# Loads of v, z and u issued by GpSimd instead of SP in a fused attention and token-mixing kernel

## The chip, the cores and the metric

The kernel runs on one core of one Trainium2 chip. The metric is the device time of one execution in microseconds (us); the time before is the median of three runs. The engines of the core are TensorE (PE, with its weight loads shown apart as PEld), VectorE (DVE), ScalarE (ACT), GpSimd (POOL) and SyncE (SP), which here only issues DMAs.

## What is computed

Two stages follow each other, for 8 batches of 3200 rows; u and v have 256 columns, z has 64.

```python
scores = (1 / S) * z @ z.T            # S = 3200
attn   = maximum(scores, 0) ** 2
x      = u * (attn @ v)               # first stage
wq, wk = x @ w_q, x @ w_k             # second stage
mixed  = (1 / 8) * (wq @ wk.T) @ x
out    = maximum(mixed, 0) @ w_out
```

All inputs and the output are float32 in DRAM. The kernel computes in float16 with float32 sums. In the second stage it uses wk.T @ x, which is only 64 x 256 ("heads"), so that no 3200 x 3200 matrix arises there.

## The kernel before, in words

**Tiling.** A batch has 25 tiles of 128 rows (NT). Its columns of the score matrix are cut into seven groups (NG): six of 512 and one of 128 (`widths`). For a group, score tiles of 128 rows by 512 columns are made in pairs by PE (`scores`, L307) into PSUM. `first_stage` turns a pair into g = 4 max(score, 0), on DVE (L321) or on ACT (L319). `second_stage` squares g into a float16 tile `at`, on POOL (L332) or on ACT (L330). PE then uses the `at` tiles as weights against v (`second_product`, emitted at L369) and sums into two PSUM banks `acc`. Since the score matrix is symmetric, some blocks of `at` are turned by DMA transposes on SP (L351, tiles `tt` and `ts`) and used again in a later group instead of being computed twice.

**Gate.** When a group is complete, `gate` multiplies `acc` by u into the float16 tile `x_sb`: half of it on DVE straight from PSUM (L507), the other half copied out by ACT (L506) and multiplied on POOL (L509). The last, narrow group goes by L499 to L502. `x_sb` is turned by a DMA transpose on SP (L518) for the second stage.

**Order.** Everything is written out by hand. A loop counts phases k; the engines get their instructions in the order in which the Python code emits them, and each engine and each DMA queue runs its own in that order. In a phase some two or three score pairs are made while the squares of an earlier phase are consumed (`LAG = 2`). The opening and the ending have lists of their own. `due(k, fn)` has a function called at the start of phase k; `asides` holds functions that are called later in the same phase.

**Loads.** For batch 0, z comes in four pieces through SP and is cast by three engines (`cast_first`, L121), and v comes in four pieces by DMAs that POOL issues and that cast on the way (`load_first_v`, L112). For batches 1 to 7:

- z comes in two pieces and v in seven. `load_piece` (L144 to L153) takes a float32 buffer `piece` out of the pool `pst` (three buffers), has SP load it (L147), and some phases later (3, 4 or 5) casts it into `zr` or `v_sb` (L151): on POOL in even phases, on ACT in odd ones. `V_FIRST` and `V_LATER` give the phase of each load of v and the delay of its cast.
- z is then turned by DMA transposes on SP (`turn_z`, L176), and parts are copied by ACT (`spread_z`, L184 and L188).
- u comes in float32, one piece for each group, into one of two buffers (`load_u`, L195, issued by SP). The load of the next group's u is put into `to_load` when a group begins, and it is emitted at the front of the phase after that, behind `turn_x`. Its buffer was last read by the gate of the group before.

`v_sb` has two buffers, one for each of two batches; `zr` has one.

**SP's queue.** So SP issues the transposes of `at`, `x_sb`, z and the keys (`kx`, L551), the loads of z, v and u, and the stores of the output (L740, L783, L1318). Each waits in that order for what it needs.

Of the kernel before, what the change touches and what calls it, by code (L numbers as in the profile page):

```python
# [10 lines left out]
FP32 = mybir.dt.float32  # L11
# [5 lines left out]
def kernel(  # L17
# [10 lines left out]
    nc = tc.nc  # L28
# [4 lines left out]
    P = 128  # L33
    NT = S // P
# [21 lines left out]
    px = ctx.enter_context(tc.tile_pool(name="px", bufs=7))  # L56
    pk = ctx.enter_context(tc.tile_pool(name="pk", bufs=1))
    pxt = ctx.enter_context(tc.tile_pool(name="pxt", bufs=4))
    pst = ctx.enter_context(tc.tile_pool(name="pst", bufs=3))
    pu = ctx.enter_context(tc.tile_pool(name="pu", bufs=2))  # L60
    pg = ctx.enter_context(tc.tile_pool(name="pg", bufs=7))
    pfo = ctx.enter_context(tc.tile_pool(name="pfo", bufs=2))
# [28 lines left out]
    zT, vs, us, xs, xTs, qks, ks, hacc, hss, rts, zds = ({} for _ in range(11))  # L91

    def rows(t, b):
        return t[b].rearrange("(p n) d -> p n d", n=NT)
# [5 lines left out]
    zr = pz.tile([P, NT + 1, dqk], FP16, tag="zr", name="zr")  # L100
# [37 lines left out]

    V_FIRST = [(13, 3), (14, 3), (15, 3), (16, 3), (17, 3), (18, 3), (19, 3)]
    V_LATER = [(7, 5), (9, 4), (11, 4), (13, 3), (14, 3), (15, 3), (17, 4)]

    def load_piece(k, b, src, dst, n0, nn, later):  # L144
        d = src.shape[2]
        piece = pst.tile([P, nn, d], FP32, tag="piece", name="piece")
        nc.sync.dma_start(out=piece[:], in_=rows(src, b)[:, n0 : n0 + nn, :])  # L147

        def cast():
            copy = nc.gpsimd.tensor_copy if now[0] % 2 == 0 else nc.scalar.copy  # L150
            copy(out=dst()[:, n0 : n0 + nn, :], in_=piece[:])  # L151

        due(k + later, lambda: asides.append(cast))  # L153

    def load_v(k, b, n0, nn):
        if n0 == 0:
            vs[b] = pv.tile([P, NT, D], FP16, tag="v_sb", name="v_sb")
        load_piece(k, b, v, lambda: vs[b], n0, nn, (V_FIRST if b == 1 else V_LATER)[n0 // 4][1])

    def load_z(k, b, n0, nn):  # L160
        load_piece(k, b, z, lambda: zr, n0, nn, 4)

    def z_at(b, half):
        return P if b > 0 and half == 0 else 0
# [4 lines left out]
    def turn_z(b, n0, nn):  # L173
        if n0 == 0:
            zT[b] = pzt.tile([P, S + P], FP16, tag="zT2", name="zT2")
        nc.sync.dma_start_transpose(  # L176
            out=z_tiles(b)[:, n0 : n0 + nn, 1, :],
            in_=zr[:, 2 * n0 : 2 * (n0 + nn), :].rearrange("p n k -> p (n k)"),
        )

    def spread_z(b, half, n0, n1):
        low, high = slice(0, dqk), slice(dqk, P)
        if half == 0:
            nc.scalar.copy(  # L184
                out=z_tiles(b)[low, n0 + 1 : n1 + 1, 0, :], in_=z_tiles(b)[high, n0:n1, 1, :]
            )
        else:
            nc.scalar.copy(  # L188
                out=z_tiles(b)[high, n0:n1, 0, :], in_=z_tiles(b)[low, n0:n1, 1, :]
            )  # L190

    def load_u(b, gi):
        n0, nn = starts[gi] // P, widths[gi] // P
        us[b, gi] = pu.tile([P, 4, D], FP32, tag="u_sb", name="u_sb")
        nc.sync.dma_start(out=us[b, gi][:, 0:nn, :], in_=rows(u, b)[:, n0 : n0 + nn, :])  # L195


    wqk = consts.tile([P, ND, 2, dh], FP16, tag="wqk", name="wqk")
# [590 lines left out]
    keyed, keyed_at, to_turn, to_spread, asides = [], [-9], [], [], []  # L789
    hTs, to_turn_heads = {}, []  # L790

    def due(k, fn):
        at_phase.setdefault(k, []).append(fn)
# [72 lines left out]
    def group_begun(k, b, gi):  # L866
        following = (b, gi + 1) if gi + 1 < NG else (b + 1, 0)
        if (b, gi) == (0, 0):
            due(k + 5, lambda: load_u(*following))
        elif following[0] < B:  # L870
            to_load.append(following)
        if gi == 0 and b + 1 < B:
            for i, (n0, nn) in enumerate([(0, 16), (16, NT - 16)]):
                at = k + (5 if b == 0 else 1) + i
                due(at, lambda at=at, n0=n0, nn=nn: load_z(at, b + 1, n0, nn))
            for i, n0 in enumerate((0, 5, 9)):
                due(k + (10 if b == 0 else 6) + i, lambda n0=n0: turn_z(b + 1, n0, 5 if n0 == 0 else 4))
            n = NT // 2
            for i, (half, n0, n1) in enumerate(
                [(0, 0, n // 2), (1, 0, n // 2), (0, n // 2, n), (1, n // 2, n + 1)]  # L880
            ):
                due(
                    k + (14 if b == 0 else 13) + i,
                    lambda half=half, n0=n0, n1=n1: spread_z(b + 1, half, n0, n1),
                )
            for i in range(-(-NT // 4)):
                at = k + (V_FIRST if b == 0 else V_LATER)[i][0]
                due(at, lambda at=at, i=i: load_v(at, b + 1, 4 * i, min(4, NT - 4 * i)))

    last = B - 1  # L890
    first_kx = list(kxs)
    now = [0]
    mixed_at = [-9]
    make_identity(nc, ident)
    due(3, lambda: load_u(0, 0))
    due(6, load_weights)
    due(8, load_out_weights)
# [91 lines left out]
    def opening(order):  # L989
        sc, g = {}, {}  # L990
        for word in order.split():
            what, n, by = word[0], int(word[1:2]), word[2:]
            if what == "z":
                cast_first(n, int(by[0]), by[1])
            elif what == "t":
                turn_first(n)
            elif what == "c":
                place_first(n, by)
            elif what == "v":
                load_first_v(*[(0, 4), (12, 6), (18, 7), (4, 8)][n])  # L1000
            elif what == "s":
                sc[n] = scores(2 * n)
            elif what == "e":
                g[n] = first_stage(2 * n, sc.pop(n), by == "A")
            elif what == "q":
                each(second_stage(2 * n, g.pop(n), by == "A"))
            elif what == "w":
                warm(2 * int(word[1:]))
            elif what == "u":
                load_u(0, 0)  # L1010
            elif what == "m":
                ti = [t for x in tiles[2 * n : 2 * n + 2] for t in x[2]]
                for fn in whole(second_product(0, 0, ti, n == 0, False)):
                    fn()
        return [(2 * n, g[n]) for n in sorted(g)]
# [4 lines left out]
    made_by = [4, 10, 16]  # L1020
    produced, consumed, k = 16, 6, 3
    group_begun(1, 0, 0)
    steps = 6
    across = False
# [3 lines left out]
    while groups:  # L1028
# [71 lines left out]
        b, gi = groups[0]  # L1100
        if begins:
            group_begun(k, b, gi)
            need = ends[b, gi]
            scored = tiles[consumed:need]
            scored = [t for _, _, tis in scored for t in tis]
            left = [t for t in range(NT) if t not in scored]
# [247 lines left out]
```

## Time and profile before

| | |
|---|---|
| median of 3 runs | 765.52 us (765.5 to 765.67) |
| profiled execution, first to last instruction (its own time is given only as this span) | 763.7 us |
| busy: PE / DVE / ACT / POOL | 754.3 / 461.9 / 551.1 / 537.1 us |
| mean granted clock of TensorE | 0.998 |
| DMA packets | 289614, 150.23 MB |
| read from and written to HBM | 59.38 and 26.21 MB |

How to read the lines below: in the list of groups, a row gives the line, the engine, the operation, output<-input with their shapes, the count, then the busy time in us and the mean duration of one in ns, and then the engine's idle time just ahead of them with what ended most of it. In the list of waits, a row names who waited for whom, the us in total, the times and the longest. In a timeline, a row gives the start, the time until the end of the last one, the engine, line and operation and the count. In the table of stretches, a row gives the stretch, its length, the engine's busy time (and instructions), the granted clock, the mean busy share of the 16 DMA engines and GB/s. A row of DMA issues ends with the size of one and the median us from issue to landing. SPq is SP's queue.

### The profile page before, as it was taken

The numbers are of one execution on the slowest core, as the hardware profiler recorded it, in microseconds if no ns is written. First come the engines' busy times: TensorE is split into PE (matmuls) and PEld (weight loads), VectorE is DVE, ScalarE is ACT, GpSimd is POOL, SyncE is SP. The second block draws the span as 40 slices with busy tenths as digits, with TensorE's granted clock in tenths as the row PEclk, the third lists the DMA queues.
The fourth block names the chain that finished last, engine by engine and source line by source line (L and its number), as shares of the span: only waits on it lengthen the run. The fifth ranks groups of instructions, "written<-read, shape, count | busy, mean of one in ns | idle before, by whom it ended". The sixth has DMA issues, their size and how long they took to land.

```text
span 763.7 us, 29059 instructions
## 1 busy us (share of the span) xinstructions
PE 754.3 (99%) x12888; PEld 618.0 (81%) x12888; DVE 461.9 (60%) x458; ACT 551.1 (72%) x651; POOL 537.1 (70%) x351
## 2 busy tenths in 40 slices
PE   9999999999999999999999999999999999999996
PEld 6777888888888887888888888888878888888884
DVE  7655676546755567555665557656566565755534
ACT  8666776677767777687776877759777697776555
POOL 7897797768766678676787668866688665854540
PEclk9999999999999999999999999999999999999999
DMA  8999789887999969997899998999899999798636
GB/s 178 189 197 219 187 187 192 174 181 160 206 196 233 219 166 185 221 235 195 214 177 219 243 195 181 158 228 265 135 223 189 228 250 156 161 222 193 176 74 262
DMA packets 289614, 150.23 MB, mean 197 GB/s; under 512 B 265168, under 2 KB 268752, under 8 KB 289488
## 3 DMA queue, kind: packets, MB, share of 16 engines
q1 hardware_dynamic: 288768, 146.48, 91.2%
q0 software_dynamic: 576, 1.64, 1.1%
q8 instruction: 100, 1.64, 0.9%
q14 instruction: 26, 0.21, 0.1%
q10 hardware_dynamic: 144, 0.26, 0.1%
HBM read 59.38 MB, written 26.21 MB: 112 GB/s over the span
## 4 chain that ended last, share of the span: by engine, by line
PE 97%; DVE 2%; issue 0%; DMA 0%; ACT 0%; DVEq 0%; ACTq 0%
PE acc L369 72%; PE sc L307 12%; PE fo L369 5%; PE qk L369 5%; PE mx L657 1%; DVE x_sb L507 1%; DVE fo L1312 0%; DVE g L321 0%; PE ztp L130 0%; DMA z<-in_z_dram 0%; PE qk L610 0%; DVE zT L136 0%; PE xtx L634 0%; PE hd L644 0%; ACT fo L1316 0%
## 5 line engine op out<-in xcount | busy, mean ns | idle before, releaser
L321 DVE TENSOR_SCALAR g<-sc 128x1024 f32<-128x1024 f32 x329 | 400.5, 1223 | 240.5 <-PE sc L307 225.9
L332 POOL TENSOR_TENSOR at<-g 128x1024 f16<-128x1024 f32 x229 | 431.4, 1893 | 131.1 <-DVE g L321 106.5
L369 PE MATMUL acc<-v_sb,at 64*128 64x256 f16 (+1 forms) x7187 | 461.8, 269 | 1.6 <-DVE x_sb L507 0.5
L369 PEld LDWEIGHTS <-at 64*128 64x128 f16 (+1 forms) x7187 | 353.9, 94 | 86.9 <-PE acc L369 25.4
L330 ACT ACTIVATE at<-g 128x1024 f16<-128x1024 f32 x227 | 236.1, 1056 | 14.3 <-DVE g L321 7.2
L369 PE MATMUL acc<-v_sb,tt 64*128 64x256 f16 x2552 | 178.7, 269 | 0.0
L307 PE MATMUL sc<-zT 64*128 64x512 f16 (+1 forms) x1008 | 165.3, 357 | 0.2
L319 ACT ACTIVATE g<-sc 128x1024 f32<-128x1024 f32 x127 | 130.0, 1024 | 45.5 <-PE sc L307 43.2
L369 PEld LDWEIGHTS <-tt 64*128 64x128 f16 x2552 | 130.1, 94 | 14.2
L509 POOL TENSOR_TENSOR x_sb<-gt,u_sb 128x512 f16<-128x512 f32 x48 | 61.2, 1276 | 66.2 <-ACT gt L506 61.8
L678 ACT ACTIVATE rt<-mx 128x1024 f16<-128x1024 f32 x47 | 47.9, 1024 | 32.6 <-PE mx L657 32.5
L506 ACT COPY gt<-acc 128x512 f32<-128x512 f32 x48 | 28.0, 584 | 46.5 <-PE acc L369 44.7
L307 PEld LDWEIGHTS <-zT 64*128 64x128 f16 x1008 | 51.9, 94 | 8.8 <-issue 1.7
L369 PE MATMUL fo<-wo,rt 64*128 64x256 f16 (+1 forms) x696 | 57.9, 270 | 0.0
L544 ACT CAST qk<-qk 128x512 f16<-128x512 f32 x47 | 27.5, 585 | 34.3 <-PE qk L369 31.6
L369 PEld LDWEIGHTS <-rt 64*128 64x128 f16 (+1 forms) x696 | 35.5, 94 | 15.3 <-PE fo L369 6.3
L507 DVE TENSOR_TENSOR x_sb<-acc,u_sb 128x512 f16<-128x512 f32 x48 | 33.2, 691 | 20.3 <-PE acc L369 19.5
L739 ACT ACTIVATE fo<-fo 128x1024 f32<-128x1024 f32 x39 | 39.9, 1024 | 1.9 <-PE fo L369 1.7
L369 PEld LDWEIGHTS <-x_sb 64*128 64x128 f16 x672 | 29.8, 95 | 4.5 <-PE qk L369 0.9
L369 PE MATMUL qk<-kx,x_sb 64*128 64x64 f16 x672 | 32.8, 190 | 0.0
L369 PE MATMUL qk<-xT_sb,wkq 64*128 64x512 f16 (+3 forms) x118 | 25.8, 326 | 0.0
L369 PE MATMUL qk<-xT_sb,wqk 64*128 64x384 f16 (+3 forms) x148 | 24.8, 296 | 0.0
(86 smaller groups left out, 275.2 us busy)
## 6 DMA issues: line engine op xcount, KB each, us to landing
u_sb<-in_u_dram SPq DMA_DIRECT2D x48, 512.0 KB, 5.5
out_dram<-fo SPq DMA_DIRECT2D x43, 512.0 KB, 4.1
piece<-in_v_dram SPq DMA_DIRECT2D x42, 512.0 KB, 5.2
piece<-in_z_dram SPq DMA_DIRECT2D x7, 512.0 KB, 5.2
tt<-at SPq DMA_TRANSPOSE x162, 4.6
out_dram<-fo SPq DMA_DIRECT2D x9, 256.0 KB, 2.9
piece<-in_z_dram SPq DMA_DIRECT2D x7, 288.0 KB, 4.9
u_sb<-in_u_dram SPq DMA_DIRECT2D x8, 128.0 KB, 4.2
```

What stands on the lines that cost most here:

```text
L307: nc.tensor.matmul(out=sc[:, h, at : at + w], lhsT=zT[b][half : half + dqk, ds(z_at(b, h) + ti * P, P)], rhs=zT[b][half : half + dqk, ds(z ...
L319: nc.scalar.activation(out=g[:], in_=sc[:], func=RELU, scale=GSCALE)
L321: nc.vector.tensor_scalar(out=g[:], in0=sc[:], scalar1=0.0, scalar2=GSCALE, op0=AOP.max, op1=AOP.mult)
L330: nc.scalar.square(out=out, in_=g[:])
L332: nc.gpsimd.tensor_mul(out=out, in0=g[:], in1=g[:])
L369: return nc.tensor.matmul(out=self.out, lhsT=self.lhsT(rows), rhs=self.rhs(rows), start=start, stop=stop)
L506: nc.scalar.copy(out=upper[:], in_=accs[1][:])
L507: nc.vector.tensor_mul(out=x[:, 0:n], in0=accs[0][:, 0:n], in1=ug[:, 0:n])
L509: nc.gpsimd.tensor_mul(out=x[:, n : 2 * n], in0=upper[:], in1=ug[:, n : 2 * n])
L544: nc.scalar.copy(out=qks[b, gi][:, 0:gw], in_=out)
L678: nc.scalar.activation(out=out, in_=ps[:], func=RELU)
L739: nc.scalar.mul(out=flat_out[:, sl], in_=part, mul=FINAL_SCALE)
```

## The change

The float32 staging is removed: the pool `pst`, `load_piece` and its casts. v and z are loaded by DMAs that POOL issues and that write float16 straight into `v_sb` and `zr`. u is still loaded as float32, but its DMA is issued by POOL as well. The phases in which the loads are emitted stay the same. SP's queue keeps the transposes, the first loads of z and the weights, and the stores.

```diff
-    pst = ctx.enter_context(tc.tile_pool(name="pst", bufs=3))
...
-    V_FIRST = [(13, 3), (14, 3), (15, 3), (16, 3), (17, 3), (18, 3), (19, 3)]
-    V_LATER = [(7, 5), (9, 4), (11, 4), (13, 3), (14, 3), (15, 3), (17, 4)]
-
-    def load_piece(k, b, src, dst, n0, nn, later):
-        d = src.shape[2]
-        piece = pst.tile([P, nn, d], FP32, tag="piece", name="piece")
-        nc.sync.dma_start(out=piece[:], in_=rows(src, b)[:, n0 : n0 + nn, :])
-
-        def cast():
-            copy = nc.gpsimd.tensor_copy if now[0] % 2 == 0 else nc.scalar.copy
-            copy(out=dst()[:, n0 : n0 + nn, :], in_=piece[:])
-
-        due(k + later, lambda: asides.append(cast))
-
-    def load_v(k, b, n0, nn):
+    V_FIRST = [13, 14, 15, 16, 17, 18, 19]
+    V_LATER = [7, 9, 11, 13, 14, 15, 17]
+
+    def load_v(b, n0, nn):
         if n0 == 0:
             vs[b] = pv.tile([P, NT, D], FP16, tag="v_sb", name="v_sb")
-        load_piece(k, b, v, lambda: vs[b], n0, nn, (V_FIRST if b == 1 else V_LATER)[n0 // 4][1])
-
-    def load_z(k, b, n0, nn):
-        load_piece(k, b, z, lambda: zr, n0, nn, 4)
+        nc.gpsimd.dma_start(out=vs[b][:, n0 : n0 + nn, :], in_=rows(v, b)[:, n0 : n0 + nn, :])
+
+    def load_z(b, n0, nn):
+        nc.gpsimd.dma_start(out=zr[:, n0 : n0 + nn, :], in_=rows(z, b)[:, n0 : n0 + nn, :])
...
     def load_u(b, gi):
         n0, nn = starts[gi] // P, widths[gi] // P
         us[b, gi] = pu.tile([P, 4, D], FP32, tag="u_sb", name="u_sb")
-        nc.sync.dma_start(out=us[b, gi][:, 0:nn, :], in_=rows(u, b)[:, n0 : n0 + nn, :])
+        nc.gpsimd.dma_start(out=us[b, gi][:, 0:nn, :], in_=rows(u, b)[:, n0 : n0 + nn, :])
```

The calls of `load_z` and `load_v` in `group_begun` lose the argument that told the phase.

More of the change, by code (lines that the diff above doesn't have):

```diff
@@ L874, in group_begun @@
                 at = k + (5 if b == 0 else 1) + i
-                due(at, lambda at=at, n0=n0, nn=nn: load_z(at, b + 1, n0, nn))
+                due(at, lambda n0=n0, nn=nn: load_z(b + 1, n0, nn))
             for i, n0 in enumerate((0, 5, 9)):
@@ L886, in group_begun @@
             for i in range(-(-NT // 4)):
-                at = k + (V_FIRST if b == 0 else V_LATER)[i][0]
-                due(at, lambda at=at, i=i: load_v(at, b + 1, 4 * i, min(4, NT - 4 * i)))
+                at = k + (V_FIRST if b == 0 else V_LATER)[i]
+                due(at, lambda i=i: load_v(b + 1, 4 * i, min(4, NT - 4 * i)))
     last = B - 1
```

## The prediction

> **What bounds the kernel now.** I read the page's busy line and its chain first, then the busy time of TensorE by stretches of the span, then who waited for whom on TensorE's weight loads.
>
> ```profile
> PE 754.3 (99%) x12888; PEld 618.0 (81%) x12888; DVE 461.9 (60%) x458; ACT 551.1 (72%) x651; POOL 537.1 (70%) x351
> ...
> PE 97%; DVE 2%; issue 0%; DMA 0%; ACT 0%; DVEq 0%; ACTq 0%
> ```
>
> ```profile
> 0.00:20.00 20.00, 18.77 (x207) 1.00 0.85 183
> 20.00:60.00 40.00, 39.59 (x650) 1.00 1.10 195
> 60.00:740.00 680.00, 678.83 (x11902) 1.00 0.94 196
> 740.00:763.70 23.70, 17.07 (x139) 0.95 0.62 222
> ```
>
> ```profile
> PEld L369 <- PE acc L369: 25.4, 106, 0.3
> ...
> PEld L369 <- POOL at L332: 0.2, 1, 0.2
> ```
>
> The reader is to see that the matrix engine (PE) is the bound from end to end: 97% of the chain is PE, and from 60 to 740 us it is idle for 680.00 - 678.83 = 1.17 us in all. Its larger idle times stand at the two ends, where the change moves little. A matmul's shown time covers its pipeline, so gaps of up to 0.3 us hide in "busy"; most of these are PE waiting for itself (25.4 us). GpSimd (POOL) kept PE waiting once, for 0.2 us. So removing work from other engines can give little here, and only what makes PE wait can cost. PE's own instructions and their order are the same in both compiled programs.
>
> **The change, part by part.** What leaves and what comes:
>
> ```profile
> L151 POOL CAST v_sb<-piece 128x1024 f16<-128x1024 f32 (+1 forms) x24 | 23.0, 957 | 0.0
> L151 POOL CAST zr<-piece 128x1024 f16<-128x1024 f32 (+1 forms) x7 | 6.1, 878 | 0.0
> ...
> L112 POOL DMA_DIRECT2D v_sb<-in_v_dram x4 | 2.3, 579 | 0.1
> ```
>
> ```profile
> L151 ACT CAST v_sb<-piece 128x1024 f16<-128x1024 f32 (+1 forms) x25 | 23.4, 935 | 0.0
> ...
> L151 ACT CAST zr<-piece 128x576 f16<-128x576 f32 (+1 forms) x7 | 5.8, 826 | 0.0
> ```
>
> ```profile
> u_sb<-in_u_dram SPq DMA_DIRECT2D x48, 512.0 KB, 5.5
> ...
> piece<-in_v_dram SPq DMA_DIRECT2D x42, 512.0 KB, 5.2
> piece<-in_z_dram SPq DMA_DIRECT2D x7, 512.0 KB, 5.2
> ...
> piece<-in_z_dram SPq DMA_DIRECT2D x7, 288.0 KB, 4.9
> u_sb<-in_u_dram SPq DMA_DIRECT2D x8, 128.0 KB, 4.2
> piece<-in_v_dram SPq DMA_DIRECT2D x7, 128.0 KB, 3.9
> ```
>
> *Casts.* ScalarE (ACT) loses 25 + 7 = 32 casts, 23.4 + 5.8 = 29.2 us. POOL loses 24 + 7 = 31 casts, 23.0 + 6.1 = 29.1 us. PE was not waiting for any of them, so I take no gain; at the very most it is the 1.17 us above.
>
> *Issues.* 48 + 42 + 7 + 7 + 8 + 7 = 119 loads leave SP's queue and are issued by POOL. POOL's only issues in this trace are the four first loads of v: 579 ns each on average, 528 to 720 below, at a time when few transposes ran. Under load the nearest row is that of the same u loads on SP:
>
> ```profile
> L112 POOL DMA_DIRECT2D v_sb<-in_v_dram x4: 528/534/720, 1.5 to 7.2; - x4
> ...
> DMA to landing us min/median/max: 4.5/5.4/6.4
> ```
>
> ```profile
> L195 SPq DMA_DIRECT2D u_sb<-in_u_dram x56: 338/570/1638, 14.8 to 729.9; - x56
> ...
> DMA to landing us min/median/max: 3.2/5.3/9.1
> ```
>
> So one issue costs POOL between 0.34 and 1.64 us; I take 0.58, POOL's own mean, which SP's median (0.57) agrees with. That is 119 x 0.58 = 69 us on POOL, less 29 for the casts: POOL goes from 537 to about 577 us, ACT from 551 to 522. For the steady part:
>
> ```profile
> 9.00:60.00 51.00, 45.67 (x39) 1.00 1.05 192
> 60.00:618.00 558.00, 413.21 (x256) 1.00 0.97 200
> ```
>
> From 60 to 618 us, six batches, POOL idles 558 - 413 = 145 us, 24 per batch. A batch brings 7 u + 7 v + 2 z = 16 issues, 9.3 us, and drops some 4.4 casts, 4.2 us: 5 us more against 24 idle. On average this is hidden. From 9 to 60 us only 5.3 us are idle. That is where I look closely.
>
> *The opening.* POOL squares score tiles there back to back (L332), and PE loads the squares as weights:
>
> ```profile
> 10.18 15.02 POOL L332 TENSOR_TENSOR at<-g 128x1024 f16<-128x1024 f32 x8 [2.42 <-ACT g L319]
> 25.15 1.29 POOL L509 TENSOR_TENSOR x_sb<-gt,u_sb 128x512 f16<-128x512 f32 x1
> ```
>
> ```profile
> 14.04 1.90 POOL L332 TENSOR_TENSOR at<-g 128x1024 f16<-128x1024 f32 x1
> ```
>
> ```profile
> 16.25 0.11 PEld L369 LDWEIGHTS <-at 64*128 64x128 f16 x2
> ```
>
> ```profile
> 26.38 1.91 POOL L332 TENSOR_TENSOR at<-g 128x1024 f16<-128x1024 f32 x1
> ```
>
> ```profile
> 30.04 0.10 PEld L369 LDWEIGHTS <-at 64*128 64x128 f16 x2
> ```
>
> The eight squares end at 25.20. From the third's start (14.04) the pace is (25.20 - 14.04 - 1.90) / 5 = 1.85 us. Two paces back from 14.04 is 10.34, so 0.16 us was idle ahead of the second square. In the new compiled order, u's first load stands between squares one and two; a u load and a z load between six and seven; the second z load behind the gate L509, ahead of square nine; another u load behind that. With p for an issue, squares two to six are late by p - 0.16, seven and eight by 3p - 0.16, nine by 4p - 0.16. The third square ended at 15.94, and the weight load that waits for it by the program's semaphores ran at 16.25: 0.31 us to spare. With p = 0.58 it is 0.42 late, so PE waits 0.11. The ninth ended at 28.29 and is loaded at 30.04: 1.75 to spare, 2.16 late, so 0.41, of which 0.11 was already lost: 0.30 more. **Opening: +0.41 us.** Other squares there have more to spare. VectorE (DVE) waits for squares too, because they free its output buffers:
>
> ```profile
> DVE g L321 <- PE sc L307: 225.9, 253, 2.5
> ...
> DVE g L321 <- POOL at L332: 2.5, 3, 1.0
> ```
>
> I cost that at nothing, since DVE then waits less for PE's scores (225.9 us in all). If that cover fails, DVE passes on the 1.6 us by which squares seven and eight are late.
>
> *Start of a batch.* There u, z, u are issued behind the last small gate, z again two squares later:
>
> ```profile
> 98.06 1.04 POOL L151 CAST v_sb<-piece 128x1024 f16<-128x1024 f32 x1
> 99.06 11.15 POOL L332 TENSOR_TENSOR at<-g 128x1024 f16<-128x1024 f32 x6
> ```
>
> ```profile
> 102.76 1.89 POOL L332 TENSOR_TENSOR at<-g 128x1024 f16<-128x1024 f32 x1
> ```
>
> ```profile
> 106.33 0.10 PEld L369 LDWEIGHTS <-at 64*128 64x128 f16 x2
> ```
>
> The cast (1.00 until the next start) is gone, four issues come: the third square of this run is late by 4p - 1.00 = 1.32 us and has 106.33 - 104.65 = 1.68 to spare. No stall; one begins at p = 0.67.
>
> *Waits that move.* A u load on POOL waits for both halves of an earlier gate; POOL's own half stands ahead of it in the same queue, so this is over when POOL gets there. Behind it are the squares, whose cost is counted. The load lands within 6.4 us (row above) and is read a group later, 763.7 / 56 = 13.6 us. v is loaded a batch ahead. z's transposes wait for the load instead of for a cast, which ends earlier. SP issues 119 DMAs less, and its transposes stand behind no load: I cost that at nothing, as PE's waits list no transpose.
>
> *Sum.* 763.7 + 0.41 = 764.1 us of span. The profiled execution's own time is shown only as its span; the median of the runs, 765.52, is 1.8 us above it, which I take as what lies around it. **765.9 us.**
>
> **The rivals.**
>
> *The issue costs more under load (slower).* All four of POOL's rows are from the first 8 us, and SP's issues reach 1.64. With p = 1.0, square nine is 3.84 late against 1.75: 2.1 us; the batch start at 97 us gives 4.0 - 1.0 - 1.68 = 1.3. If the six others give a quarter of that each, 2.0, the sum is 5.4: 770.9 us. It decides from p = 0.67 up. POOL as a whole would become the bound only at (24 + 4.2) / 16 = 1.76 us, above every row. Against it: POOL's and SP's medians.
>
> One mechanism would be that DVE keeps POOL from writing descriptors. In the opening both overlap:
>
> ```profile
> 7.23 0.53 POOL L112 DMA_DIRECT2D v_sb<-in_v_dram  x1
> ```
>
> ```profile
> 7.63 0.94 DVE L121 CAST zd<-z 128x448 f16<-128x448 f32 x2
> ```
>
> This cast reads and writes SBUF, and the issue was no longer than its neighbours. An issue that waited for half a DVE instruction L321 (1223 ns) would have p = 0.58 + 0.61 = 1.2, and the opening alone would cost 4.8 - 0.16 - 1.75 = 2.9. The Trainium skill, "SBUF — State Buffer", section "SBUF: two separate sides", warns of this: a DMA issued by GpSimd starves for descriptors while VectorE runs a copy in a two-port mode. By that rule the steady instructions here, which read PSUM, would leave p alone; only such casts would stretch it, and the row above shows no stretch.
>
> *The transposes suffer.* In one queue a transpose waits its turn behind a load; in two they share the DMA engines.
>
> ```profile
> q1 hardware_dynamic: 288768, 146.48, 91.2%
> ```
>
> The DMA share is 0.94 from 60 to 740 us (row above), so 6% more time per byte would make DMA the pace, and each per cent past that costs 6.8 us: 1% past is 772.7. Against it: the bytes hardly change, v's landing from POOL (5.4) is that from SP (5.2), and PE has no wait for a transpose.
>
> *The casts' time comes back.* If ACT, freed of 29 us, empties PSUM earlier, PE's idle time in the middle goes: 765.5 - 1.2 + 0.4 = 764.7; at most, with the opening's loss hidden, 764.3. More would have to come out of gaps inside PE's "busy".
>
> **How the numbers follow.** The forecast has 0.57, the dearer issue 0.24, the transposes 0.09, the casts 0.10, of which I give 0.06 to over 0.2%, since the hidden gaps are larger than the idle time. 0.2% is 1.5 us, about what a measurement of this kernel can tell from no change. The forecast and the small gain lie inside it: 0.57 + 0.04 = 0.61. Slower has 0.33, faster 0.06. The range goes from 764.5, just below the gain, to 772, which takes in the dear issue; the forecast's own is 765.3 to 766.8, for p from 0.53 to 0.72.
>
> **What would show it.** The issues on POOL should read near 0.55 us through the whole span, POOL's busy time near 577, ACT's near 522. PE's busy time from 60 to 740 us should fall short by no more than 1.5 us, and its new waits should be for "POOL at" between 16 and 31 us. It is wrong if POOL's issues are near 1 us and such waits stand at every batch start, if PE waits for transposes, or if "DVE x_sb" or "ACT gt" wait for a u load.

## The result, and the profile after

| | median us | lowest to highest | ratio to before, 95% interval |
|---|---|---|---|
| before (4 runs) | 765.51 | 765.36 to 765.67 | |
| after (4 runs) | 776.58 | 769.30 to 780.83 | 1.0131 [1.009, 1.0171] |

The change makes the kernel 1.3% slower, and its time, which was the same within 0.3 us in these runs, now scatters over 11 us. The ratios here and below leave out executions that a comparison takes for disturbed, while the medians and ranges count all, so that of a kernel that scatters by itself the median can stand higher than its ratio. The profile of after is that of its quickest run, 769.3 us with a span of 767.5: it shows 3.8 us of the loss, and a second profile, of the same kernel run again (e8, span 775.2), shows 11.5.

The page of after, its busy line and its chain, and the busy time of TensorE from 60 to 740 us:

```profile
PE 753.9 (98%) x12888; PEld 617.6 (80%) x12888; DVE 462.0 (60%) x458; ACT 526.8 (69%) x619; POOL 575.1 (75%) x439
...
PE 93%; POOL 2%; DMA 1%; ACT 1%; DVE 1%; issue 1%; ACTq 0%; DVEq 0%; POOLq 0%
```

```profile
60.00:740.00 680.00, 675.52 (x11871) 1.00 0.99 175
```

PE does the same work, but in the steady part it is idle for 680.00 - 675.52 = 4.48 us where it was idle for 1.17. That alone is 3.3 of the 3.8 us. Who waited for whom, in after:

```profile
POOL at L316 <- DMA tt<-at: 20.1, 9, 7.6
...
ACT at L314 <- DMA tt<-at: 8.4, 6, 2.0
ACT at L314 <- DMA ts<-at: 4.6, 1, 4.6
...
PE acc L353 <- ACT gt L490: 2.4, 1, 2.4
...
PEld L353 <- POOL at L316: 0.8, 3, 0.4
```

The first rows are new. The squares on POOL and ACT wait for DMA transposes: a square writes into one of 11 `at` buffers, and the buffer is not free until the transpose that reads it has landed. The transposes themselves, by their tile, before and then after (ns that an issue took SP, shortest, median and longest; us from issue to landing):

```profile
L351 SPq DMA_TRANSPOSE tt<-at x162: 1195/1373/4432, 13.1 to 719.6; - x162
...
DMA to landing us min/median/max: 2.5/4.6/9.7
```

```profile
L335 SPq DMA_TRANSPOSE tt<-at x162: 1192/1728/6304, 12.8 to 723.4; - x162
...
DMA to landing us min/median/max: 2.6/5.4/13.2
```

SP has 119 loads less to issue, and yet its transposes cost it more time (all 317 of them, of every tile: 501.0 us before, 570.6 after) and land later. For `tt` the median moves by 0.8 us, the longest by 3.5. How such a one reaches PE is read from the chain of after around its longest stall,

```profile
437.97 0.18 ACT zT L172
438.15 7.17 DMA tt<-at
...
445.53 0.58 ACT gt L490
446.11 0.04 issue
446.15 2.14 PE acc L353 x36
```

and ACT's timeline at the same place:

```profile
444.57 1.06 ACT L314 ACTIVATE at<-g 128x1024 f16<-128x1024 f32 x1 [4.62 <-DMA ts<-at]
445.53 0.57 ACT L490 COPY gt<-acc 128x512 f32<-128x512 f32 x1
```

ACT stands idle for 4.62 us, because its next square needs a buffer that a late transpose (`ts`) still reads. The chain names another one of that moment, a `tt` that was issued at 438.15 and landed 7.17 us later, at 445.32. Behind that square stands the gate's copy out of PSUM (L490), and PE can't begin its next sum before that copy. PE is idle for 2.4 us (the wait row above). It never waits for the transpose by name.

In the run of 775.2 us the same path is longer. Its chain, and TensorE in stretches of 5 us:

```profile
420.55 13.73 DMA tt<-at
...
435.26 1.04 ACT at L314
436.30 0.48 ACT gt L490
436.78 0.04 issue
436.82 4.00 PE acc L353 x35
```

```profile
430.00:435.00 5.00, 2.56 (x43) 1.00 1.12 142
435.00:440.00 5.00, 3.18 (x31) 0.59 1.15 192
440.00:445.00 5.00, 5.00 (x64) 0.73 0.97 205
445.00:450.00 5.00, 5.00 (x100) 1.00 1.16 228
```

The transpose lands after 13.73 us, and PE is idle for 2.44 + 1.82 = 4.3 us in the first two stretches. Then comes a second price: the granted clock is 0.59 in the stretch of the stall's end and 0.73 in the next, in which PE gets through 64 matmuls in 5 us, and through 100 in the 5 us after that. (Not every stall is followed by a slower clock, as is shown further down.) Over the whole execution PE's idle time is 775.2 - 757.6 = 17.6 us against 763.7 - 754.3 = 9.4 before, and its busy time is 3.3 us longer for the same instructions: 8.2 + 3.3 = 11.5 us, about what stalls and what the slowed clock cost.

### The profile page after: what moved, and what is told of

Read it like the earlier page. It is cut to its first block, busy times and chain, and to the rows that moved or that the text cites. A ratio compares the mean times of both kernels' runs of the same rounds, so it can differ in the third digit from the quotient of the medians.

```text
span 767.5 us, 29007 instructions
## 1 busy us (share of the span) xinstructions
PE 753.9 (98%) x12888; PEld 617.6 (80%) x12888; DVE 462.0 (60%) x458; ACT 526.8 (69%) x619; POOL 575.1 (75%) x439
## 3 DMA queue, kind: packets, MB, share of 16 engines
q1 hardware_dynamic: 271632, 91.58, 70.7%
q0 software_dynamic: 16944, 42.20, 26.8%
## 4 chain that ended last, share of the span: by engine, by line
PE 93%; POOL 2%; DMA 1%; ACT 1%; DVE 1%; issue 1%; ACTq 0%; DVEq 0%; POOLq 0%
PE acc L353 69%; PE sc L291 12%; PE fo L353 5%; PE qk L353 5%; POOL at L316 2%; PE mx L641 1%; DMA tt<-at 1%; DVE x_sb L491 1%; ACT g L303 0%; DMA z<-in_z_dram 0%; ACT at L314 0%; DVE fo L1296 0%; PE qk L594 0%; POOL x_sb L493 0%; ACT gt L490 0%
## 5 line engine op out<-in xcount | busy, mean ns | idle before, releaser
L314 ACT ACTIVATE at<-g 128x1024 f16<-128x1024 f32 x227 | 236.1, 1055 | 27.5 <-DVE g L305 13.5
L490 ACT COPY gt<-acc 128x512 f32<-128x512 f32 x48 | 28.1, 585 | 46.5 <-PE acc L353 46.5
L179 POOL DMA_DIRECT2D u_sb<-in_u_dram x56 | 31.5, 562 | 3.6 <-issue 1.8
L146 POOL DMA_DIRECT2D v_sb<-in_v_dram x49 | 28.7, 586 | 0.0
```

What stands on the lines that cost most here:

```text
L146: nc.gpsimd.dma_start(out=vs[b][:, n0 : n0 + nn, :], in_=rows(v, b)[:, n0 : n0 + nn, :])
L179: nc.gpsimd.dma_start(out=us[b, gi][:, 0:nn, :], in_=rows(u, b)[:, n0 : n0 + nn, :])
L314: nc.scalar.square(out=out, in_=g[:])
```

## The experiments

The theories: **A**, loads in a queue of their own run beside SP's transposes and make them late, and the `at` buffers pass it on; **B**, POOL's time for the issues; **C**, the cast inside the DMA. Later: **D**, it is the bytes beside the transposes, in any queue but SP's; **E**, it is GpSimd's queue; **F**, the bytes make the transposes late and POOL, without its idle time, can't catch up; **G**, small DMAs, or GpSimd's own queue, did what F claims. Before was run with each group on the same chip: 765.37 to 765.61 us. Lines of a helper shift by a few in kernels with added lines.

| | what is changed | median us | ratio, 95% interval |
|---|---|---|---|
| e1 | after, 16 `at` buffers | 777.45 | 1.0105 [1.0073, 1.0137] |
| e2 | before, u by GpSimd | 770.15 | 1.0061 [1.004, 1.0083] |
| e3 | after, u by SP | 765.78 | 1.0002 [0.9993, 1.001] |
| e4 | before, 119 small DMAs by GpSimd | 765.93 | 1.0003 [0.9995, 1.0012] |
| e5, e14 | after, u by ScalarE | 769.96, 771.43 | 1.0054 [1.0041, 1.0067], 1.0069 [1.0039, 1.01] |
| e6 | after, u two phases later | 776.79 | 1.0161 [1.0133, 1.0189] |
| e7 | before, u by ScalarE | 767.38 | 1.0033 [1.002, 1.0046] |
| e8 | after again | 775.83 | 1.013 [1.0106, 1.0154] |
| e9 | e5 and 56 small DMAs by GpSimd | 774.37 | 1.011 [1.0077, 1.0144] |
| e10 | after, a quarter of u's bytes | 765.34 | 0.9997 [0.9988, 1.0006] |
| e11 | e3 and 56 small DMAs by GpSimd | 766.52 | 1.0024 [1.0008, 1.004] |
| e12 | after, 25 squares from POOL to ACT | 785.25 | 1.0229 [1.0197, 1.0261] |
| e13 | e5 and 56 memsets on POOL | 769.31 | 1.0048 [1.0031, 1.0065] |

**e1, more buffers.**

```diff
-    NAT = 11
+    NAT = 16
```

> The changed kernel with 16 instead of 11 buffers for the squared tiles at, in the room that the staging left. Theory A (the loads in a second queue run beside the transposes and slow them; a transpose that still reads an old at buffer then keeps GpSimd and ScalarE from writing a new square, and in the end TensorE): the transposes on SP stay slow (about 570 us of issue time, landing near 5.4 us), but waits for 'DMA tt<-at' on GpSimd fall from 20 us to under 5, and the time falls to 765 to 768 us with little scatter. Theory B (GpSimd's own 69 us of issuing make its squares late): buffers do not help, time stays at 769 to 781 us. Theory C (the cast inside the DMA makes the loads land late): as B.

Measured: 777.45 us (766.7 to 792.25), ratio 1.0105. A's 765 to 768 us is missed. In its profiled run (span 788.6) the squares wait for transposes for only 4.8 us (33.1 in after), but now PE waits for transposes by name:

```profile
PE acc L353 <- issue: 6.7, 3, 4.2
PE qk L353 <- DMA xT_sb<-x_sb: 6.3, 1, 6.3
PE acc L353 <- DMA tt<-at: 3.2, 1, 3.2
```

```profile
210.00:215.00 5.00, 0.83 (x12) 0.79 1.11 111
215.00:220.00 5.00, 5.00 (x60) 0.52 1.40 105
```

So the buffers are one way by which the lateness reaches PE, and not its cause: with that way opened, it arrives by another. The transposes still cost SP 604.9 us. The two stretches show the clock again, 0.79 and 0.52 around a stall of 4.2 us (5.00 - 0.83).

**e2, e3 and e4: the parts.** e2 is before with u alone moved; e3 is after with u back on SP; e4 is before with a DMA of 16 bytes a row into scratch, issued by GpSimd at each of the 119 places.

```diff
 # e2, load_u of before
-        nc.sync.dma_start(out=us[b, gi][:, 0:nn, :], in_=rows(u, b)[:, n0 : n0 + nn, :])
+        nc.gpsimd.dma_start(out=us[b, gi][:, 0:nn, :], in_=rows(u, b)[:, n0 : n0 + nn, :])
 # e3, load_u of after
-        nc.gpsimd.dma_start(out=us[b, gi][:, 0:nn, :], in_=rows(u, b)[:, n0 : n0 + nn, :])
+        nc.sync.dma_start(out=us[b, gi][:, 0:nn, :], in_=rows(u, b)[:, n0 : n0 + nn, :])
 # e4, before, called in load_piece and load_u
+    def small(src):
+        tiny = pdm.tile([P, 4], FP32, tag="tiny", name="tiny")
+        nc.gpsimd.dma_start(out=tiny[:], in_=src[:, 0, 0:4])
```

> The kernel before with only u's 56 loads issued by GpSimd; v and z stay with SP, staging and casts. Theory A: u is 27 of the 53 MB that move to the second queue, so about half of the loss, 769 to 773 us, and GpSimd or ScalarE waiting for 'DMA tt<-at' by some 10 us. Theory B: 56 issues and no cast removed, GpSimd busy about 569 us, so nearly the whole loss, 771 to 777 us, with new waits for 'POOL at' and not for transposes. Theory C: no cast in any of these DMAs, so 765 to 767 us.

> The changed kernel with u's loads given back to SP; v and z stay with GpSimd and are cast on the way. Theory A: about half of the loss, 769 to 773 us. Theory B: 63 issues (36 us) against 29 us of removed casts, GpSimd busy about 544 us, so almost no loss, 765 to 767 us. Theory C: the whole loss, 774 to 779 us.

> The kernel before with every load where it was, and beside each of the 119 a small extra DMA issued by GpSimd at the same place (128 rows of 16 bytes into a scratch tile that nobody reads). It adds GpSimd's issue time (119 times about 0.57 us, with no cast removed: busy about 605 us) and almost no bytes. Theory A: 765.5 to 767.5 us, transposes as before (SP's issue time for them near 501 us). Theory B: as much as the change or more, 774 to 785 us, with TensorE waiting for 'POOL at'. Theory C: 765.5 to 767 us.

Measured: u alone costs 0.61%; v and z with their casts in the DMA cost nothing (e3); 119 issues, which bring POOL to 600.0 us busy, cost nothing (e4). B is inside its range in e3 but fails in e4 (and narrowly in e2), and C fails in e2 and e3: both fall as causes by themselves. A is right in e2 and e4, but not in e3, where it expected about half of the loss: loads in a queue of their own are not enough. The loss needs u's loads out of SP's queue, and v and z in another queue make it about twice as large. Why v and z alone do no harm there, no run shows. One difference is on the page of after: a load of u by GpSimd moves 512 KB, one of v 256 KB.

**e5, e7 and e14: which queue.** u's loads by ScalarE, in after (e5 and, later, e14) and in before (e7).

```diff
 # e5 and e14, load_u of after
-        nc.gpsimd.dma_start(out=us[b, gi][:, 0:nn, :], in_=rows(u, b)[:, n0 : n0 + nn, :])
+        nc.scalar.dma_start(out=us[b, gi][:, 0:nn, :], in_=rows(u, b)[:, n0 : n0 + nn, :])
 # e7, load_u of before
-        nc.sync.dma_start(out=us[b, gi][:, 0:nn, :], in_=rows(u, b)[:, n0 : n0 + nn, :])
+        nc.scalar.dma_start(out=us[b, gi][:, 0:nn, :], in_=rows(u, b)[:, n0 : n0 + nn, :])
```

> The changed kernel, but u's 56 loads are issued by ScalarE instead of GpSimd; v and z stay with GpSimd. Theory D (two queues: SP's single queue held the loads back behind the transposes; any other queue lets a load of u out beside the transposes that TensorE needs soonest, their landings get a tail of over 10 us, TensorE stalls for several us, and its granted clock then falls to about a half for some us): as slow as the changed kernel, 770 to 780 us, with landings of transposes up to 12 us or more. Theory E (it is GpSimd's queue that is bad for u: its packets of 4 KB take 231 ns against 203 from SP): 765 to 767 us, landings at most 10 us. ScalarE's issues (56 x 0.5 us or so) are paid out of its idle time in both.

> The kernel before, but u's 56 loads are issued by ScalarE; v and z stay with SP and are cast as before. No DMA of the steady part comes from GpSimd. Theory D: as slow as u alone on GpSimd (770.15 measured), 768 to 772 us. Theory E: 765 to 766.5 us.

> The run with u on ScalarE's queue once more, as the reference on the same chip: 768 to 772 us by both theories (769.96 the first time, with single executions up to 782.89).

Measured: 1.0033 in before, 1.0054 and 1.0069 in after. Another queue than SP's costs time even where GpSimd issues nothing in the steady part, as D has it. But e5 (769.96) and e7 (767.38) are just below D's ranges, though above E's: by ScalarE u costs about half of what it costs by GpSimd, so E is not refuted as an addition. ScalarE's own time for the 56 issues (338 ns each in e5 and e7) was not tried without u's bytes, as GpSimd's was in e4, so what part it has in these losses is open. The longest landing of a `tt` in e5 is 13.5 us, as in after, so the tail alone doesn't tell the two apart.

**e6 and e8: the moment, and after again.**

```diff
 # e6, group_begun of after
-            to_load.append(following)
+            due(k + 3, lambda: load_u(*following))
```

> The changed kernel, but each load of u is emitted two phases later (about 8 us), still on GpSimd and still some 6 us or more ahead of its use. Theory D in its form 'the moment': u leaves now at the moment when the gate has just written x_sb and its transpose and the keys' follow; two phases later it meets less urgent ones: 765 to 769 us. Theory D in its form 'any load of u in flight beside transposes, whenever': 770 to 780 us, as the changed kernel. Theory E: 770 to 780 us as well.

> The changed kernel itself once more, beside the three others on the same chip. Both theories: 769 to 781 us from run to run, as the first time (776.58), with stalls of TensorE of 2 to 7 us at a few places that differ from run to run.

Measured: e6 776.79 us, e8 775.83. D in its form "the moment" falls: some 8 us later the loads do the same harm. e8 gives the first result again; its profile was read above.

**e10, the bytes.** After, with the same 56 issues by GpSimd; from the third load on only 64 of u's 256 columns come, and the rest of the tile keeps an earlier group's values.

```diff
-        us[b, gi] = pu.tile([P, 4, D], FP32, tag="u_sb", name="u_sb")
-        nc.gpsimd.dma_start(out=us[b, gi][:, 0:nn, :], in_=rows(u, b)[:, n0 : n0 + nn, :])
+        us[b, gi] = u_two[(b * NG + gi) % 2]
+        d = D if (b, gi) in ((0, 0), (0, 1)) else D // 4
+        nc.gpsimd.dma_start(out=us[b, gi][:, 0:nn, 0:d], in_=rows(u, b)[:, n0 : n0 + nn, 0:d])
```

> The changed kernel with a quarter of u's bytes: the same 56 issues on GpSimd, but from the third load on only 64 of 256 columns of u are loaded (the rest of the tile keeps an earlier group's u, so this part of the computation is left out). If the bytes beside the transposes are the cause (theories D and E): 765 to 768 us, landings of transposes back to at most about 10 us. If GpSimd's issue or its place in the queue is the cause (theory F without bytes): 774 us or more.

Measured: 765.34 us, ratio 0.9997 [0.9988, 1.0006], and the scatter is gone (765.16 to 766.66). The longest landing of a `tt` is 11.3 us, of an `xT_sb` 9.5, a little more than expected. The issue, by line, the squares' waits for transposes, and PE's steady part in e10; last, PE's steady part in e3:

```profile
L182 POOL DMA_DIRECT2D u_sb<-in_u_dram x56 | 41.8, 746 | 2.5 <-POOL x_sb L496 1.5 <-issue 1.0
```

```profile
ACT at L317 <- DMA tt<-at: 1.4, 2, 1.2
```

```profile
60.00:740.00 680.00, 678.84 (x11906) 1.00 0.89 149
```

```profile
60.00:740.00 680.00, 677.39 (x11886) 1.00 0.98 176
```

The issues are even dearer here (746 ns; after has 562), POOL is busier than in after, the squares wait for transposes for 1.4 us (33.1 in after), and PE's 678.84 us are before's 678.83. What went is three quarters of the bytes: a load of a full group still goes in packets of 4096 bytes, 32 instead of 128 of them, each put together from rows of 256 bytes. The DMA engines are also less busy (0.89). That the lighter load alone isn't the reason is shown by e3: it moves all of the bytes, with u in SP's queue, at a share of 0.98, and its median loses nothing. e2, e3 and e10 together show the cause: u's bytes, moved by a queue that isn't SP's.

**e9, e11, e12 and e13: POOL's time.** Why do the same bytes cost twice as much by GpSimd as by ScalarE? e9 and e11 have GpSimd issue 56 loads of 16 bytes a row at u's places, while u comes by ScalarE or SP. e12 gives POOL time back. e13 takes POOL's time without any DMA.

```diff
 # e9 (on e5) and e11 (on e3), load_u
+        tiny = pdm.tile([P, 4], FP32, tag="tiny", name="tiny")
+        nc.gpsimd.dma_start(out=tiny[:], in_=rows(u, b)[:, n0, 0:4])
 # e12, on after
-            second_on_act = [False, True, k % 2 == 0]
+            second_on_act = [False, True, k % 2 == 0 or k % 6 == 3]
 # e13 (on e5), load_u
+        nc.gpsimd.memset(idle[:], 0.0)
```

> As the run with u on ScalarE's queue (769.96 us), and GpSimd also issues 56 loads of 16 bytes a row into a scratch tile, where the changed kernel has it issue u: GpSimd's instructions are then those of the changed kernel, only u's bytes come by ScalarE's queue. Theory F (the 56 x 0.58 us that the issues take of GpSimd cost nothing alone, as 119 small ones showed, but do once transposes land late, since GpSimd then can't catch up): 774 to 780 us. Theory E (bytes that leave by GpSimd's own queue do more harm than by ScalarE's): 769 to 772 us.

> As the run with only v and z on GpSimd (765.78 us), and GpSimd also issues the 56 loads of 16 bytes a row at u's place: GpSimd is as busy as in the changed kernel, but u's bytes stay in SP's queue. Theories D and E: 765.5 to 766.8 us. Theory F in its strict form (GpSimd's lost idle time itself): 768 us or more.

> The changed kernel with 25 of its squares moved from GpSimd to ScalarE (one in every sixth phase), 25 x 1.9 = 47 us off GpSimd and 25 x 1.06 = 26 us on ScalarE, which brings both to about what they had before the change (528 and 553 us). Theory F (u's bytes make the transposes late, and GpSimd without its idle time passes the lateness on): 768 to 772 us, about that of u on ScalarE's queue. If GpSimd's idle time has no part, and u's bytes are the whole cause: 775 to 780 us as the changed kernel. If ScalarE's squares come at bad moments it is slower than that, and the run decides nothing.

> As the run with u on ScalarE's queue (769.96 us), and GpSimd clears a scratch tile of 128x544 float16 (about 0.56 us, from the row of 128x512 with 528 ns) at each of the 56 places where the changed kernel has it issue u. No DMA is added. Theory F (GpSimd's time passes the lateness of the transposes on): 773 to 779 us, as with the small DMAs (774.37). Theory G (the small DMAs, or the bytes' way through GpSimd's own queue, did the harm): 769 to 772 us, as its reference.

Measured: e9 774.37 us spoke for F. e11, 766.52, is inside the range of D and E, with a small loss (1.0024): four of its twelve executions took 769.5 to 770.8 us, while none of e3's took more than 766.9. e12 came out at 785.25, slower than after: POOL has its time back (528.8 us busy) and waits for transposes more than ever,

```profile
POOL at L316 <- DMA tt<-at: 54.7, 11, 11.6
```

so, as said beforehand, moved squares come at other moments and the run decides nothing. e13 decides. Its memset beside after's issue, both by line:

```profile
L183 POOL MEMSET idle<- 128x544 f16 x56 | 31.5, 562 | 0.1
```

```profile
L179 POOL DMA_DIRECT2D u_sb<-in_u_dram x56 | 31.5, 562 | 3.6 <-issue 1.8 <-POOL x_sb L493 1.8
```

The same 31.5 us of POOL at the same places give 769.31 us, no more than e5 and e14 without them. F falls: it isn't POOL's time. That leaves something about DMAs issued by GpSimd itself, of which even small ones seem to do some harm when the transposes are already late (e9 1.011 against e13 1.0048 and e5 1.0054; its interval touches neither, but it touches that of e14, so this is likely and not shown). What it is, no run here shows; it stays open.

## Why the prediction was wrong, point by point

The forecast was 765.9 us, with a range up to 772; the measured median is 776.58.

**The bound.** Right, and still so: PE is 93% of the chain. That is why a few stalls are nearly the whole loss.

**Issues and casts.** Right in size. u's issues took 562 ns (row above), the forecast was 580; POOL is at 575.1 us (577 forecast) and ACT at 526.8 (522). The casts' removal brought nothing (e3), and "the issue costs more under load" did not come. The Trainium skill, "SBUF — State Buffer", section "SBUF: two separate sides", warns that VectorE in a two-port mode can starve GpSimd's DMAs of descriptors; no issue of after shows a sign of it, as the longest of the 123 took 707 ns. u's loads landed after up to 11.7 us, where the prediction had 6.4 at most, and still no gate waited for one.

**The opening.** In the first 60 us PE's weight loads wait for POOL's squares twice, 0.6 us (of the 0.8 above), where before they didn't: close to the +0.41. e10 has the same two waits there and no measurable loss at the end.

**The step that failed** is this sentence: "SP issues 119 DMAs less, and its transposes stand behind no load: I cost that at nothing, as PE's waits list no transpose." Both halves of it misled. The term was not nothing: the 317 transposes cost SP 570.6 us instead of 501.0, the longest `tt` landed after 13.2 us instead of 9.7, the squares of POOL and ACT waited 33.1 us for transposes instead of 4.8, and PE lost 3.3 us of its steady part even in the quickest run, 2.4 of them in the stall that was followed above.

The first half took SP's queue for what a transpose waits in. But the packets of both queues take the time of the same 16 DMA engines: in after SP's have 70.7% of it and GpSimd's 26.8%. I grouped the transposes of seven traces by the loads and stores in flight between issue and landing (median us to landing, and their number). Other transposes were in flight nearly always, also in the first column:

```
                            no load or store   u alone     u and v
before, all by SP           3.23 (31)          3.91 (43)   4.86 (37)
e3, v and z by POOL         3.45 (30)          4.12 (24)   5.43 (50)
e7, u by ACT                3.30 (31)          4.39 (45)   5.51 (46)
e2, u by POOL               3.25 (31)          4.44 (37)   5.65 (56)
after, all by POOL          3.46 (19)          4.58 (29)   6.11 (75)
e13, u by ACT, rest POOL    3.27 (25)          4.02 (24)   6.12 (63)
e5, u by ACT, rest POOL     3.32 (24)          4.12 (26)   6.69 (67)
```

Without a load or store beside it, a transpose takes about the same time in all of them. Beside u alone the queue does not decide: 3.9 and 4.1 us with u in SP's queue, 4.0 to 4.6 in another. Beside u and v it is 4.9 us with all loads in SP's queue, 5.4 to 5.7 with some of them elsewhere, and 6.1 to 6.7 with all of them elsewhere. The packets of 256 bytes, of which SP's transposes are made, took 26.9 ns on average before and 28.7 after, and the slowest hundredth of them 99 ns and more before, 192 and more after; e3, which loses nothing, stands between (28.2 and 169). The Trainium skill, "DMA: Bandwidth & Descriptors", section "Queues, rings and completion order", says that each DMA engine takes turns between the queues that have work for it. The last column agrees with that. That one queue protects the older transposes, because a load issued behind them in the same queue lets them pass while one from another queue mixes into them, is argued from this; no run isolates the order within a queue, and why u does more harm than v stays open.

The second half looked for the price at the wrong engine. PE's list of waits in before has no transpose, but a row of another engine did:

```profile
ACT at L330 <- DMA tt<-at: 4.8, 2, 3.2
```

ACT's squares had already waited twice for late transposes, once for 3.2 us, and the gate's copy stands in the same queue. The reserve of this path was used up at times before the change, and the row was to be read as a warning.

**The rival "the transposes suffer"** was the right one, with 0.09. Its price was worked out as throughput: DMA becomes the pace past a share of 1, 6.8 us for each per cent. At that price it did not decide. The share did rise, from 0.94 to 0.99 in after and 1.03 in e5 (60 to 740 us), although fewer bytes were moved (175 GB/s instead of 196), and the runs that lost most have the highest. But e3 at 0.98 loses 1.4 us in its profiled run and nothing in the median, e2 at 0.97 loses 6.7, and e13 at 1.01 only 2.6. The loss goes with the tail. Of the 317 transposes of a profiled execution, so many landed after more than 10 us, beside its span:

```
            before  e4     e7     e10    e3     e2     e11    after
over 10 us  0       0      0      1      4      5      6      10
span, us    763.7   763.9  764.3  763.5  765.1  770.4  765.4  767.5

            e13     e5     e14    e8     e9     e1     e6     e12
over 10 us  11      13     14     16     18     21     27     28
span, us    766.3   768.8  769.7  775.2  772.0  788.6  773.6  785.9
```

The two go up together, though not in step: a late one can stop PE for some us, and which ones do differs from run to run (the longest stall ends at 446 us in after and at 437 in e8), hence the scatter. The arguments against it (the same bytes, the same landing of v) speak of averages, and of the loads instead of the transposes.

**What the prediction left out** is the clock. The stall of after, 2.4 us at 446 us, left the granted clock alone. One of 3.5 us in e2, and one of only 2.0 us in e5 (37.6 to 39.7 us), did not. Stretches after these stalls, of after, e2 and e5:

```profile
445.00:450.00 5.00, 3.85 (x74) 1.00 0.97 234
```

```profile
115.00:120.00 5.00, 5.00 (x62) 0.64 1.09 241
```

```profile
40.00:45.00 5.00, 4.94 (x62) 0.66 0.95 215
```

The stalls of 4.2 and 4.3 us (e1, e8) brought it to 0.52 and 0.59. In all traces of this case every stall of 3.2 us or more was followed by a slower clock, those of 2.0 to 2.8 us sometimes (e5, e9, once in e12) and sometimes not (after, another in e12), and none of 1.9 us or less. The Trainium skill, "TensorE: Matmul & The Clock Gate", section "What's actually happening", has the clock halved after an idle window of about 3.4 us, which runs freely, and restored after as much busy time. The traces agree for the long stalls. They don't show 3.4 us of idle time as the least that it takes, since the 2.0 us of e5 were enough.

## What to carry to other kernels

Before moving bulk loads out of the queue that issues latency-bound DMAs, look at how long those take to land and at who waits for their buffers: a shared queue may be the only thing that keeps the loads behind them. Follow the waits of every engine that feeds the bound one, since a late DMA reaches it through buffers and queues and not under its own name. Price such a change by the longest landings, and not by the mean or the share of busy time; a stall of TensorE of 3.2 us or more was paid twice here, in idle time and in clock, and some of 2.0 to 2.8 us were too.

## What the runs showed of the hardware that was not expected

- The granted clock falls to between 0.50 and 0.66 over 5 us at or behind the end of every stall of 3.2 us or more, and behind some shorter ones (0.66 behind one of 2.0 us in e5), while one of 2.8 us in e12 left it at 1.00. In e8 this is about 3.3 us of a loss of 11.5.
- The same loads cost this kernel more when GpSimd issues them than when ScalarE does: 1.0061 [1.004, 1.0083] against 1.0033 [1.002, 1.0046] with u alone (these two touch), 1.013 [1.0106, 1.0154] against 1.0054 [1.0041, 1.0067] and 1.0069 [1.0039, 1.01] with v and z on GpSimd in both. It isn't GpSimd's time (e13). Nor do the transposes land later by it in the profiled runs: 10 and 16 of them after more than 10 us with GpSimd (after, e8), 13 and 14 with ScalarE (e5, e14).
- An issue by GpSimd took 562 ns for u in full and 746 ns on average in e10, where most loads bring a quarter of it in pieces of 256 bytes, four times as many: here the issue goes by pieces more than by bytes.
